# Turning x by crossbar DMA for three of four head pairs in units 3 to 7, with x kept pair-major

## The chip, the cores and the metric

The kernel runs on one core of a Trainium2 chip. The metric is the device time of one execution in microseconds (us); lower is better. Before the change, three runs took 267.28, 267.41 and 268.54 us, a median of 267.41 us.

## What is computed

A block-sparse attention feeds a gated feed-forward layer. q, k and v have shape (4 batches, 8 heads, 768 positions, 64). Reduced to what matters:

```python
k_sum = k.reshape(B, H, 24, 32, D).max(axis=3)
v_sum = v.reshape(B, H, 24, 32, D).mean(axis=3)
# each query: keys less than 16 positions away, and all 24 block summaries (score + log 32)
a = softmax([masked local scores, summary scores])
attn = a @ [v, v_sum]
x = attn.transpose(0, 2, 1, 3).reshape(3072, 512)
g, val = x @ w_gate, x @ w_val               # 512 -> 1536
ffn = (gelu(g) * val) @ w_out                # 1536 -> 512
out = x + sigmoid(x @ w_res) * ffn
```

Because x stands on the left of three products, the kernel needs x twice: with tokens on the partitions (`xn`, for the last line) and with the 512 features on the partitions (`xT`, for the products). The step from `xn` to `xT` is what the change is about.

## The kernel before, in words

**Units.** The 3072 tokens are cut into eight units of 384 tokens (`TU`), two for each batch. A unit has three sub-tiles of 128 tokens (`NSUB`) and four head pairs, each of which gives 128 of the 512 features (`KO` = 4 blocks of features). The main loop (line 454) runs over u from 0 to 7. In iteration u the TensorE (PE) does the feed-forward part of unit u and, mixed into it, the attention of the next unit, n = u + 1. So the x of unit n is made and turned in iteration n - 1; the x of unit 0 is made ahead of the loop, and iteration 7 makes none.

**Feed-forward part of a unit.** For each of 12 feature blocks `fo`, `fo_step` (line 342) runs four matmuls with `w_gate` into `g` and four with `w_val` into `vv` (line 333; the contraction runs over ko = 0 to 3, one head pair of `xT` for each), a Gelu on ScalarE (ACT, line 339) and a product on VectorE (DVE, line 340). After that come, for each sub-tile, `res_step` (four matmuls with `w_res`, line 351, and a tanh, line 357), `ffn_step` (12 matmuls with `w_out`, line 367) and `end_step` (two DVE operations, lines 372 and 374, and the store of 256 KB, line 376, issued on the DMA queue of SyncE, SP). The second of the two DVE operations adds `xn`.

**Attention part.** For each head pair: `s_step` (scores, line 269, and exp, lines 275 and 278), `av_step` (the product with the values, line 301, then `av_norm`: a reciprocal, line 309, and a multiplication that writes the pair's share of `xn`, line 311), and `xt_step`, which turns that pair: three PE transposes of 128 x 128, one for each sub-tile (line 320, into the PSUM tile `xp`), and one ACT copy of 128 x 384 from PSUM to `xT` (line 322).

**Order.** Nothing reorders the work: the order in the text is the order on each engine, and each engine and queue takes its instructions one after the other. Only the semaphore waits are put in from what each instruction reads and writes, and they go by region: an ACT copy of block ko = 3 does not hold back a matmul that reads block ko = 0. In iterations 1 to 6 the order around the change is, after the 12 blocks `fo`: scores 0 and 1; res 0; ffn 0; res 1; av 0 and 1; scores 2 and 3; end 0; six matmuls of ffn 1; xt 0; the other six; xt 1; res 2; av 2 and 3; end 1; seven matmuls of ffn 2; xt 2; three matmuls; xt 3; two matmuls; end 2. Then the next iteration begins with `g` of `fo` = 0, which reads `xT` block by block, ko = 0 first. Iteration 0 has an order of its own and is not touched.

**Buffers.** `xn` and `xT` have two buffers each, so those of unit n were last used by unit n - 2. The PSUM tiles `ao` and `t` are used in turn by `av_step` and `xt_step`; the DMA needs neither.

**Other users of the DMA queues.** The loads of q, k and v for batches 1 to 3 (`load_batch`, line 166, and `load_values`, line 96) are issued by GpSimd (POOL) on its own queue; those for batches 2 and 3 are in the program at the start of iterations 1 and 3, but POOL runs ahead of the PE and issues each as soon as its buffer is free. On SP's queue lie the 26 stores and, at `fo` = 0 of iterations 2 and 4, `turn_batch` (lines 214 and 217): 12 crossbar transposes that turn k and q of batches 2 and 3. They are operations of the same kind as those that the change adds.

Of the kernel before, what the change touches and what calls it, by code (L numbers as in the profile page):

```python
# [9 lines left out]
BF16 = mybir.dt.bfloat16  # L10
AF = mybir.ActivationFunctionType
ALU = mybir.AluOpType
# [3 lines left out]
def kernel(  # L16
# [83 lines left out]
    with tc.manual_schedule():  # L100
# [156 lines left out]
        def s_step(u, hp, st, s=None, two=None, masked=True):  # L257
            b, half = u // 2, u % 2
            first = s is not None
            if two:  # L260
                s = [pool.tile([128, 512], F32, tag=tag, name="s1") for pool, tag in two]
            elif not first:
                s = ps_s.tile([128, 2, 512], F32, tag="s", name="s")
            kw, qt = kW[b % 2][hp], qT[b % 2][hp]
            for t in range(HT):
                tt = half * HT + t
                for hh in range(2):
                    ps = slice(hh * 64, hh * 64 + 64)
                    nc.tensor.matmul((s[hh] if two else s[:, hh])[:, t * QT:(t + 1) * QT], kw[ps, tt, :],  # L269
                                     qt[ps, tt * QT:(tt + 1) * QT], start=not first, stop=True,  # L270
                                     skip_group_check=True)
            P = ppool.tile([128, 2, HT, QT], BF16, tag="P", name="P")
            if two:
                for hh in range(2):
                    nc.scalar.activation(P[:, hh].rearrange("p t q -> p (t q)"), s[hh][:, 0:TU], AF.Exp,  # L275
                                         scale=scale, bias=bias_t[:])
            else:
                nc.scalar.activation(P.rearrange("p a t q -> p a (t q)"), s[:, :, 0:TU], AF.Exp,  # L278
                                     scale=scale, bias=bias_t[:])
            st["P", hp] = P  # L280
            if not first and masked:
                mask_part(hp, st)
# [23 lines left out]
        def av_norm(hp, st):  # L306
            ao = st["ao", hp]
            rz = work.tile([128, NSUB, 2, 1], F32, tag="rz", name="rz")
            nc.vector.reciprocal(rz[:], ao[:, :, :, D:D + 1])  # L309
            xn = st["xn"].rearrange("p s (h d) -> p s h d", d=D)[:, :, 2 * hp:2 * hp + 2, :]  # L310
            nc.vector.tensor_mul(xn, ao[:, :, :, 0:D], rz.to_broadcast([128, NSUB, 2, D]))  # L311

        def av_step(u, hp, st, pool=ps_o, tag="ao"):
# [3 lines left out]
        def xt_step(u, ko, st, pool, tag, copy=nc.vector.tensor_copy):  # L317
            xp = pool.tile([128, TU], BF16, tag=tag, name="xp")
            for sub in range(NSUB):
                nc.tensor.transpose(xp[:, sub * 128:(sub + 1) * 128],  # L320
                                    st["xn"][:, sub, ko * 128:(ko + 1) * 128], ident[:])
            copy(st["xT"][:, ko, :], xp[:])  # L322

        def new_unit():
            return {"xn": upool.tile([128, NSUB, DM], BF16, tag="xn", name="xn"),
                    "xT": upool.tile([128, KO, TU], BF16, tag="xT", name="xT")}

        def half_fo(st, w, fo, lo, hi, acc=None):
# [41 lines left out]
        def end_step(u, st, sub, c0=0, c1=DM):  # L370
            f, th = st["f", sub], st["th", sub][:, c0:c1]
            nc.vector.scalar_tensor_tensor(th, th, 1.0, f[:, 0:c1 - c0], ALU.add, ALU.mult)  # L372
            o = work.tile([128, DM], F32, tag="o", name="o")
            nc.vector.scalar_tensor_tensor(o[:, 0:c1 - c0], th, 0.5, st["xn"][:, sub, c0:c1], ALU.mult, ALU.add)  # L374
            row = u * TU + sub * 128
            nc.sync.dma_start(out=out[row:row + 128, c0:c1], in_=o[:, 0:c1 - c0])

# [76 lines left out]
        for u in range(NU):  # L454
            b, half = u // 2, u % 2
            nb = b + 1
            n = u + 1
            if half == 1 and b + 2 < B:
                load_batch(b + 2)
            gvT = upool.tile([128, FO, TU], BF16, tag="gvT", name="gvT")  # L460
            for fo in range(FO):
                if u == 0 and fo < 2:
                    for w, _, acc in firsts[2 * fo:2 * fo + 2]:
                        half_fo(st, w, fo, KO - 1, KO, acc)
                    fo_end(gvT, fo, firsts[2 * fo][2], firsts[2 * fo + 1][2])
                else:
                    fo_step(st, gvT, fo)
                values_step(u, fo)
                if u == 0 and fo == 4:
                    vext_consts(1)  # L470
                    kw_consts(1)
                    load_batch(1)
                if half == 0 and 1 < nb < B and fo == 0:
                    turn_batch(nb)
                if half == 1 and 1 < nb < B and 0 < fo <= NP:
                    k_rest(kW[nb % 2][fo - 1])
                if u == 1 and fo < 8:
                    home = TT if fo % 2 else AO
                    hp, kq = fo % NP, fo // NP
                    if kq:  # L480
                        q_step(q_sb[nb], nb, 0, S, hp, *home)
                    else:
                        k_step(nb, hp, *home)
                if u == 0 and fo >= FO - 2:
                    for hp in range(2 * (fo - FO + 2), 2 * (fo - FO + 2) + 2):
                        q_step(qb, 0, TU, S, hp, *(TT if hp % 2 else AO))
            nst = new_unit() if n < NU else None
            if u == 0:
                s_step(n, 0, nst)
                s_step(n, 1, nst, two=(AO, TT))  # L490
                r = [res_part(st, sub) for sub in range(NSUB)]
                tanh_part(st, 0, r[0])
                tanh_part(st, 1, r[1])
                tanh_part(st, 2, r[2])
                ffn_step(st, gvT, 0, 0, 4)
                av_step(n, 0, nst, *AO)
                av_step(n, 1, nst, *TT)
                s_step(n, 2, nst)
                s_step(n, 3, nst, two=(MM, MM))
                ffn_step(st, gvT, 1, 0, 4)  # L500
                xt_step(n, 0, nst, *AO, nc.scalar.copy)
                xt_step(n, 1, nst, *TT, nc.scalar.copy)
                ffn_step(st, gvT, 0, 4, 8)
                av_step(n, 2, nst, *AO)
                av_step(n, 3, nst, *TT)
                ffn_step(st, gvT, 1, 4, 8)
                ffn_step(st, gvT, 2, 0, 4)
                xt_step(n, 2, nst, *AO, nc.scalar.copy)
                xt_step(n, 3, nst, *TT, nc.scalar.copy)
                ffn_step(st, gvT, 2, 4, 8)  # L510
                for sub in range(NSUB):
                    ffn_step(st, gvT, sub, 8, FO)
                    end_step(u, st, sub)
                st = nst
                continue
            if nst is None:
                for sub in range(NSUB - 1):
                    res_step(st, sub)
                    ffn_step(st, gvT, sub, 0, FO)
                    end_step(u, st, sub)  # L520
                res_step(st, NSUB - 1)
                for c0, c1 in ((0, 256), (256, 384), (384, DM)):
                    ffn_step(st, gvT, NSUB - 1, 0, FO, c0, c1)
                    end_step(u, st, NSUB - 1, c0, c1)
                continue
            s_step(n, 0, nst)
            s_step(n, 1, nst, two=(AO, TT))
            res_step(st, 0)
            ffn_step(st, gvT, 0, 0, FO)
            res_step(st, 1)  # L530
            av_step(n, 0, nst, *AO)
            av_step(n, 1, nst, *TT)
            s_step(n, 2, nst)
            s_step(n, 3, nst, two=(MM, MM), masked=False)
            end_step(u, st, 0)
            mask_part(3, nst)
            ffn_step(st, gvT, 1, 0, 6)
            xt_step(n, 0, nst, *AO, nc.scalar.copy)
            ffn_step(st, gvT, 1, 6, FO)
            xt_step(n, 1, nst, *TT, nc.scalar.copy)  # L540
            res_step(st, 2)
            av_step(n, 2, nst, *AO)
            av_step(n, 3, nst, *TT)
            end_step(u, st, 1)
            ffn_step(st, gvT, 2, 0, 7)
            xt_step(n, 2, nst, *AO, nc.scalar.copy)
            ffn_step(st, gvT, 2, 7, 10)
            xt_step(n, 3, nst, *TT, nc.scalar.copy)
            ffn_step(st, gvT, 2, 10, FO)
            end_step(u, st, 2)  # L550
            st = nst
# [30 lines left out]
```

The softmax here doesn't subtract the row's maximum and nothing guards it: scores larger than these inputs give would overflow.

## Time and profile before

| what | value |
|---|---|
| median of three runs | 267.41 us |
| the profiled execution's own time | 267.3 us |
| its span, first to last instruction | 265.6 us |
| PE busy | 256.5 us (97%) |
| DVE busy | 167.3 us (63%) |
| ACT busy | 138.8 us (52%) |
| POOL busy | 80.0 us (30%) |
| granted TensorE clock | 1.000 |
| SP's queue, packets' share of the 16 DMA engines | 15.0% |
| POOL's queue, the same share | 67.5% |

"Busy" is the share of the span in which an engine had at least one instruction running. Matmuls overlap in the PE, so the distance between the starts of two successive groups says more about what an instruction costs the PE than its duration does: a duration is the time from start to end of one, a distance is what the next one had to wait. A DMA has two times: how long the issuing queue is occupied, and the time from issue to landing, when its completion is seen.

### The profile page before, as it was taken

How to read it: one execution, taken by the hardware profiler on the slowest of the kernel's cores; microseconds unless marked ns; L12 is line 12 of the kernel's file. 1: busy time of each engine (PE TensorE's matmuls, PEld its weight loads, DVE VectorE, ACT ScalarE, POOL GpSimd, SP SyncE). 2: the span in 40 equal slices, each digit the busy share in tenths (PEclk: the TensorE clock that was granted, in tenths of full speed). 3: DMA queues.
4: the chain of work that ended last, by engine and by line, in shares of the span. 5: the costliest groups of instructions: out<-in, count | busy, mean ns of one | idle time of the engine just before them, and what ended most of it. 6: DMA issues, size and time to landing. Idle time of an engine off the chain costs nothing.

```text
span 265.6 us, 5816 instructions
## 1 busy us (share of the span) xinstructions
PE 256.5 (97%) x2305; PEld 145.1 (55%) x2330; DVE 167.3 (63%) x405; ACT 138.8 (52%) x240; POOL 80.0 (30%) x107
## 2 busy tenths in 40 slices
PE   8799999999999999999999999999999999999994
PEld 2536555566545555556645555556655565556543
DVE  3744863498477877478737866578638853674424
ACT  2745449647565534744365635744365636553310
POOL 7966633998999930040000000000000000000000
PEclk9999999999999999999999999999999999999999
DMA  5999999999999999357001354121001200020012
GB/s 83 172 170 196 197 206 187 141 182 175 119 122 159 188 142 157 54 70 113 2 0 43 107 101 82 31 73 48 2 0 43 79 0 2 18 101 3 2 39 79
DMA packets 90315, 24.50 MB, mean 92 GB/s; under 512 B 76464, under 2 KB 87344, under 8 KB 90288
## 3 DMA queue, kind: packets, MB, share of 16 engines
q0 software_dynamic: 73488, 14.69, 67.5%
q1 hardware_dynamic: 16800, 9.44, 15.0%
q8 instruction: 18, 0.29, 0.5%
q14 instruction: 9, 0.07, 0.1%
HBM read 29.36 MB, written 6.29 MB: 134 GB/s over the span
## 4 chain that ended last, share of the span: by engine, by line
PE 90%; POOL 3%; DMA 3%; issue 1%; DVE 1%; ACT 1%; POOLq 0%; DVEq 0%
PE g L333 23%; PE vv L333 23%; PE f L367 23%; PE r L351 8%; PE ao L301 4%; DMA vext<-in_v_dram 3%; PE s L269 2%; PE vs L227 2%; PE xp L320 2%; POOL vext L96 2%; PE tp L176 1%; PE gv L333 1%; POOL k_sb L87 1%; PE wp L382 1%; DVE th L372 0%
## 5 line engine op out<-in xcount | busy, mean ns | idle before, releaser
L333 PE MATMUL g<-xT,w_gate 128*128 128x384 bf16 x380 | 77.8, 326 | 0.0
L333 PE MATMUL vv<-xT,w_val 128*128 128x384 bf16 x380 | 77.8, 326 | 0.0
L339 ACT ACTIVATE ge<-g 128x384 f32<-128x384 f32 x95 | 46.6, 491 | 58.7 <-DVE gvT L340 31.6
L340 DVE TENSOR_TENSOR gvT<-ge,vv 128x384 bf16<-128x384 f32 x95 | 52.0, 553 | 36.9 <-PE vv L333 33.4
L367 PE MATMUL f<-w_out,gvT 128*128 128x512 bf16 (+2 forms) x298 | 68.6, 362 | 0.7
L333 PEld LDWEIGHTS <-w_val 128*128 128x128 bf16 x384 | 37.6, 98 | 25.4 <-issue 0.5
L333 PEld LDWEIGHTS <-w_gate 128*128 128x128 bf16 x384 | 36.9, 98 | 24.7 <-issue 0.8
L367 PEld LDWEIGHTS <-gvT 128*128 128x128 bf16 x312 | 27.6, 98 | 25.6
L96 POOL DMA_DIRECT2D vext<-in_v_dram x28 | 23.5, 882 | 20.7 <-PE ao L301 20.7
L322 ACT COPY xT<-xp 128x384 bf16<-128x384 bf16 x32 | 15.0, 480 | 22.6 <-PE xp L320 22.6
L351 PE MATMUL r<-w_res,xT 128*128 128x512 bf16 x88 | 24.0, 380 | 0.4
L372 DVE SCALAR_TENSOR_TENSOR th<-th,f 128x512 f32<-128x512 f32 (+2 forms) x26 | 16.7, 642 | 11.4 <-PE f L367 8.5
L286 DVE TENSOR_TENSOR P<-P,maskt 128x768 bf16<-128x768 bf16 x28 | 15.6, 557 | 12.8 <-ACT P L278 10.1
L357 ACT ACTIVATE th<-r 128x512 f32<-128x512 f32 x24 | 14.2, 601 | 17.4 <-PE r L351 17.4
L166 POOL DMA_DIRECT2D k_sb<-in_k_dram x24 | 19.8, 861 | 10.9 <-DMA w_out<-in_moe_w_out_dram 5.2
L166 POOL DMA_DIRECT2D q_sb<-in_q_dram x24 | 19.8, 888 | 0.0
L311 DVE TENSOR_TENSOR xn<-ao,rz 128x384 bf16<-128x384 f32 x32 | 17.8, 558 | 1.1
L278 ACT ACTIVATE P<-s,bias_t 128x768 bf16<-128x768 f32 x18 | 16.2, 902 | 3.3 <-PE s L269 3.2
L374 DVE SCALAR_TENSOR_TENSOR o<-th,xn 128x512 f32<-128x512 f32 (+2 forms) x26 | 16.9, 651 | 0.9
L309 DVE RECIPROCAL rz<-ao 128x6 f32<-128x6 f32 x32 | 6.1, 190 | 18.0 <-PE ao L301 18.0
L275 ACT ACTIVATE P<-s,bias_t 128x384 bf16<-128x384 f32 x28 | 14.6, 577 | 0.0
L351 PEld LDWEIGHTS <-xT 128*128 128x128 bf16 x96 | 8.6, 98 | 8.5
(72 smaller groups left out, 205.3 us busy)
## 6 DMA issues: line engine op xcount, KB each, us to landing
out_dram<-o SPq DMA_DIRECT2D x23, 256.0 KB, 3.2
vext<-in_v_dram POOLq DMA_DIRECT2D x20, 128.0 KB, 5.8
k_sb<-in_k_dram POOLq DMA_DIRECT2D x24, 96.0 KB, 5.7
q_sb<-in_q_dram POOLq DMA_DIRECT2D x24, 96.0 KB, 4.8
w_gate<-in_moe_w_gate_dram POOLq DMA_DIRECT2D x6, 256.0 KB, 8.7
w_val<-in_moe_w_val_dram POOLq DMA_DIRECT2D x6, 256.0 KB, 8.8
w_out<-in_moe_w_out_dram POOLq DMA_DIRECT2D x3, 512.0 KB, 14.1
k_sb<-in_k_dram POOLq DMA_DIRECT2D x2, 384.0 KB, 5.8
```

The costliest lines, as they stand in the source:

```text
L96: nc.gpsimd.dma_start(out=dst, in_=v[b, :, lo:hi, :].rearrange("h p d -> p h d"))
L166: nc.gpsimd.dma_start(out=sb[b][:, h // 2, :, h % 2 * D:h % 2 * D + D], in_=src[b, h].rearrange("(c p) d -> p c d", c=NC))
L278: nc.scalar.activation(P.rearrange("p a t q -> p a (t q)"), s[:, :, 0:TU], AF.Exp, scale=scale, bias=bias_t[:])
L286: nc.vector.tensor_mul(Pf, Pf, maskt.unsqueeze(1).to_broadcast([128, 2 * HT, QT]))
L311: nc.vector.tensor_mul(xn, ao[:, :, :, 0:D], rz.to_broadcast([128, NSUB, 2, D]))
L333: nc.tensor.matmul(acc[:, 0:TU], w[:, ko, fs], st["xT"][:, ko, :], start=(ko == 0), stop=(ko == KO - 1))
L339: nc.scalar.activation(ge[:], g[:, 0:TU], AF.Gelu)
L340: nc.vector.tensor_mul(gvT[:, fo, :], ge[:], vv[:, 0:TU])
L351: nc.tensor.matmul(r[:], st["xT"][:, ko, ss], w_res[:, ko, :], start=(ko == 0), stop=(ko == KO - 1))
L367: nc.tensor.matmul(st["f", sub][:, 0:c1 - c0], gvT[:, fo, ss], w_out[:, fo, c0:c1], start=(fo == 0), stop=(fo == FO - 1))
L372: nc.vector.scalar_tensor_tensor(th, th, 1.0, f[:, 0:c1 - c0], ALU.add, ALU.mult)
L374: nc.vector.scalar_tensor_tensor(o[:, 0:c1 - c0], th, 0.5, st["xn"][:, sub, c0:c1], ALU.mult, ALU.add)
```

## The change

`xn` is laid out pair-major: [128, 4 pairs, 3 sub-tiles, 128] where it was [128, 3 sub-tiles, 512]. All its readers and writers follow: `av_norm`, the PE transposes of `xt_step`, and the last DVE operation of `end_step`, which now reads four runs of 128 elements (fewer for a narrower slice) with a stride between them. A new function `xt_dma` turns one pair with one crossbar DMA transpose issued on SP's queue: in, 128 tokens x (3 sub-tiles x 128 features); out, 128 features x 3 sub-tiles x 128 tokens, straight into `xT`. In iterations 2 to 6 (units 3 to 7) it takes the place of `xt_step` for pairs 0 to 2. Transposes 0 and 1 stand ahead of `end_step` 0, transpose 2 between `av_step` 2 and `av_step` 3. Pair 3 stays on the PE with its ACT copy, as do all four pairs of units 0 to 2.

```diff
-            xn = st["xn"].rearrange("p s (h d) -> p s h d", d=D)[:, :, 2 * hp:2 * hp + 2, :]
+            xn = st["xn"][:, hp].rearrange("p s (h d) -> p s h d", d=D)
...
-                                    st["xn"][:, sub, ko * 128:(ko + 1) * 128], ident[:])
+                                    st["xn"][:, ko, sub, :], ident[:])
...
+        def xt_dma(ko, st):
+            nc.sync.dma_start_transpose(out=st["xT"][:, ko, :].rearrange("d (s m) -> d s m", s=NSUB),
+                                        in_=st["xn"][:, ko].rearrange("p s d -> p (s d)"))
...
-            return {"xn": upool.tile([128, NSUB, DM], BF16, tag="xn", name="xn"),
+            return {"xn": upool.tile([128, KO, NSUB, 128], BF16, tag="xn", name="xn"),
...
-            nc.vector.scalar_tensor_tensor(o[:, 0:c1 - c0], th, 0.5, st["xn"][:, sub, c0:c1], ALU.mult, ALU.add)
+            nc.vector.scalar_tensor_tensor(o[:, 0:c1 - c0].rearrange("p (k d) -> p k d", d=128),
+                                           th.rearrange("p (k d) -> p k d", d=128), 0.5,
+                                           st["xn"][:, c0 // 128:c1 // 128, sub, :], ALU.mult, ALU.add)
...
             s_step(n, 3, nst, two=(MM, MM), masked=False)
+            on_pe = u < 2
+            if not on_pe:
+                xt_dma(0, nst)
+                xt_dma(1, nst)
             end_step(u, st, 0)
             mask_part(3, nst)
             ffn_step(st, gvT, 1, 0, 6)
-            xt_step(n, 0, nst, *AO, nc.scalar.copy)
+            if on_pe:
+                xt_step(n, 0, nst, *AO, nc.scalar.copy)
             ffn_step(st, gvT, 1, 6, FO)
-            xt_step(n, 1, nst, *TT, nc.scalar.copy)
+            if on_pe:
+                xt_step(n, 1, nst, *TT, nc.scalar.copy)
             res_step(st, 2)
             av_step(n, 2, nst, *AO)
+            if not on_pe:
+                xt_dma(2, nst)
             av_step(n, 3, nst, *TT)
             end_step(u, st, 1)
             ffn_step(st, gvT, 2, 0, 7)
-            xt_step(n, 2, nst, *AO, nc.scalar.copy)
+            if on_pe:
+                xt_step(n, 2, nst, *AO, nc.scalar.copy)
             ffn_step(st, gvT, 2, 7, 10)
             xt_step(n, 3, nst, *TT, nc.scalar.copy)
```

## The prediction

> **What bounds the kernel now.** I read the page first: the busy shares and the chain that ended last.
>
> ```profile
> PE 256.5 (97%) x2305; PEld 145.1 (55%) x2330; DVE 167.3 (63%) x405; ACT 138.8 (52%) x240; POOL 80.0 (30%) x107
> PE 90%; POOL 3%; DMA 3%; issue 1%; DVE 1%; ACT 1%; POOLq 0%; DVEq 0%
> ```
>
> The PE is busy for 97% and makes up 90% of the chain; by its waits it loses nothing measurable in the main loop. So whatever leaves the PE shortens the run, and whatever makes the PE wait lengthens it, one for one. What does a turning step cost the PE? Not its duration. Here is the timeline of the PE at the end of iteration 4, where unit 5 is made (start, duration, engine, line, operation).
>
> ```profile
> 175.14 1.68 PE L367 MATMUL f<-w_out,gvT 128*128 128x512 bf16 x6
> 176.66 0.33 PE L320 MATMUL xp<-ident,xn 128*128 128x128 bf16 x3
> 176.83 0.81 PE L367 MATMUL f<-w_out,gvT 128*128 128x512 bf16 x3
> 177.48 0.33 PE L320 MATMUL xp<-ident,xn 128*128 128x128 bf16 x3
> 177.65 0.59 PE L367 MATMUL f<-w_out,gvT 128*128 128x512 bf16 x2
> 178.08 0.81 PE L333 MATMUL g<-xT,w_gate 128*128 128x384 bf16 x4
> 178.73 0.81 PE L333 MATMUL vv<-xT,w_val 128*128 128x384 bf16 x4
> ```
>
> A group of three transposes is followed 0.17 us later by the next group (176.66 to 176.83, 177.48 to 177.65; over all five units the distances are 0.16 to 0.17). I use 0.163. Each transpose "lasts" 0.22 us, but costs 0.054. From the g row: four matmuls in 0.65 us, 0.1625 each; the one that reads ko = 2 starts 0.325 after the row.
>
> When is the third pair's x ready? The DVE timeline of the same iteration; the second multiplication is pair 3's.
>
> ```profile
> 175.06 0.20 DVE L309 RECIPROCAL rz<-ao 128x6 f32<-128x6 f32 x1 [1.10 <-PE ao L301]
> 175.29 0.56 DVE L311 TENSOR_TENSOR xn<-ao,rz 128x384 bf16<-128x384 f32 x1
> 175.98 0.56 DVE L311 TENSOR_TENSOR xn<-ao,rz 128x384 bf16<-128x384 f32 x1
> ```
>
> Pair 2 is ready at 175.29 + 0.56 = 175.85. Its first reader through `xT`, g with ko = 2, starts at 178.08 + 0.325 = 178.405: 2.55 us later. The same distance in the other four units is 2.545 to 2.555.
>
> Last, what a crossbar transpose takes, from the rows of the two kinds that SP already issues (occupation of the queue, minimum/median/maximum in ns) and the line on landing below each.
>
> ```profile
> L217 SPq DMA_TRANSPOSE qT<-q_sb x8: 1209/1210/1308, 93.2 to 165.8; - x8
> DMA to landing us min/median/max: 2.7/2.8/8.2
> ...
> L214 SPq DMA_TRANSPOSE kW<-k_sb x16: 1182/1206/2157, 90.2 to 163.5; - x16
> DMA to landing us min/median/max: 2.3/3.2/7.9
> ```
>
> Both occupy SP for 1.2 us. With no other traffic (iteration 4) a kW transpose, 64 x 768 elements or 96 KB, lands after 2.3 to 2.4 us, with two exceptions of 3.3 and 4.1; a qT one, 128 x 768 or 192 KB, after 2.7 to 2.8. The maxima belong to iteration 2, with POOL's loads in flight. Those loads come again, in the POOL timeline:
>
> ```profile
> 115.92 3.16 POOL L96 DMA_DIRECT2D vext<-in_v_dram  x4 [20.73 <-PE ao L301]
> ```
>
> Four value loads of batch 3 are released by the last `av_step` of iteration 2, just when that iteration's third pair would be turned. No loads come after them.
>
> **What the Trainium skill says.** "VectorE: DVE Perf Modes", section "The three transpose paths", gives 390 ns for a 128 x 128 transpose on TensorE and 1309 ns by crossbar DMA. The trace disagrees on the first in a stream of matmuls (0.054 us of PE time) and has no transpose of one block to compare with the second. "DMA: Bandwidth & Descriptors", section "Queues, rings and completion order", says that each DMA engine alternates between its queues packet by packet. The trace agrees: from 96 to 102 us, with loads on POOL's queue and transposes on SP's, both moved at once:
>
> ```profile
> q0 software_dynamic: 3838, 0.48, 142.8%
> q1 hardware_dynamic: 1865, 0.45, 60.7%
> ```
>
> 0.45 MB in 6 us is 75 GB/s for SP's queue beside the loads.
>
> **The change part by part.**
> *Removed from the PE*: 3 steps x 5 units = 15 steps x 0.163 = 2.45 us, all on the path. This is the whole possible gain, 0.9%.
> *Removed from ACT*: 15 copies x 0.48 us (row L322) = 7.2 us, worth nothing: ACT is busy for 52%. The Gelu table load follows the fourth pair's copy, which stays and moves with the PE. That copy's margin stays too: in iteration 2 it ended at 118.85, and ko = 3 was read at 118.60 + 0.49 = 119.09; both move by the same 0.5 us.
> *Layout*: the `xn` write stays at 384 elements from PSUM (0.56 us). The last DVE operation reads runs of 128; I cost it at nothing. It could lose a little (0.69 now), hidden by DVE's idle 37%; at the kernel's end the slice has 128 columns, one run. No gain, since its inputs are still f32 and bf16.
> *Added on SP*: 15 transposes at up to 1.2 us. Transposes 0 and 1 can go at about 171.0 and 172.2 in iteration 4 (xn 0 and 1 end there at 171.0 and 171.7). Behind them in SP's order stands store 0, which went at 173.52, and transpose 1 leaves SP at about 173.5: a delay under 0.1, of a store that nobody waits for. Both land by 175.1 even at qT's 2.75, 2.5 us ahead of the next g. Transpose 2 waits on pair 2's multiplication; behind it stand stores 1 and 2, which are not ready until about 177.5 (DVE's line 374 ended at 177.86, two steps of 0.163 are gone) and later. `turn_batch` stands behind store 2, and the last of its 12 was issued at 107.14 and 165.83, before transpose 0 of the same iteration. SP is clear. The value loads on POOL go 0.33 us earlier, since two removed steps precede `av_step` 3.
> *Added wait*: g with ko = 2 waits for transpose 2, and all PE work queues behind it, then ACT and DVE. Of the 2.55 us, the removed third step takes 0.163: 2.39. SP starts 0.03 us after its releaser (the store at 114.06 after DVE's end at 114.03); for the PE to resume, which no row shows apart, I set aside 0.05. So the transpose **may take 2.3 us from issue to landing** (2.39 - 0.03 - 0.05); each 0.1 beyond costs 0.1 per unit.
>
> How long does it take? It has 128 partitions in, like qT, but half its columns and bytes: three blocks of 128 x 128 for six. It can't take longer than the whole of qT alone: upper end 2.75. kW of the same bytes: 2.35. In the DMA rows of that time kW's data flow from 1.1 to about 2.0 us after issue, and 0.4 passes until landing. kW and qT occupy SP equally long with the same six blocks of columns; if that goes by blocks, three halve it and the landing drops towards 1.9. I take **2.2**, between: hidden in units 4 to 7, by a small margin.
>
> In unit 3 the data phase (116.04 + 0.03 + 1.1 = 117.2) meets the first value loads, whose packets began at 117.5 before, so 117.2 after. At 75 GB/s, 96 KB take 1.3 us where kW alone took 0.9 and I expect 0.6: 0.4 to 0.7 more, so about 2.9 and a stall of 0.65. Ends: 0, if it slips in ahead; 6.6 (the first kW of iteration 2, with a store ahead of it), a stall of 4.3.
>
> *Sum*: -2.45 + 0.65 = -1.8 us. The profiled execution took 267.3 us (span 265.6 and 1.7 around it), which gives 265.5; it lies 0.1 below the median, 267.41, which gives **265.6 us**.
>
> **The rivals.**
> *B, the third transpose lands late everywhere.* If it behaves like kW or worse (2.4 to 2.75), units 4 to 7 stall by 0.1 to 0.45 each, 0.4 to 1.8 together, and unit 3 by 1.0 to 1.2. Net from 1.05 faster to 0.55 slower: 266.4 to 268.0, 267.1 in the middle. For it: equal bytes took 2.35 already. Against it: half the blocks.
> *C, slower: unit 3's transpose sits behind the value loads.* At 6.6 us it stalls by 4.3, and with transposes as long as qT the other four add 1.8: -2.45 + 6.1 = +3.65, about 271 us. It decides from stalls of 2.45 + 1.34 = 3.8 us in all. For it: landings of 6 to 8 us beside loads in iteration 2. Against it: those stood behind a store and one another; here SP's queue is empty.
> *D, nothing stalls*, the transpose staying ahead of the loads: -2.45, 265.0 us.
>
> **How the numbers follow.** Mine 0.50 (own range 265.0 to 266.4, for unit 3's stall between 0.1 and 1.4), B 0.28, C 0.13, D 0.09. A measurement tells about 0.5%, 1.34 us, from no change: below 266.07 counts as faster, above 268.75 as slower. Faster: nearly all of mine (0.43) and D, 0.52. Slower: C and an edge of B that unforeseen waits push over, 0.15. Within: 0.33. The range takes D's foot and B's end: 264.9 to 268.0, leaving out C and little else.
>
> **What would show it.** Right: 51 transposes on the PE for 96; no PE idle ahead of g in iterations 4 to 7; one wait of PE g on DMA of some 0.6 us near 118.5; landings near 2.2. Wrong: five such waits (B), or one of over 3 us (C). An SP issue well over 1.2 us, or DVE's line 374 well over 0.69 us, would be a cost that I haven't counted.

## The result, and the profile after

The changed kernel takes 271.39 us, the median of four runs (270.11 to 271.74), against 267.57 us for the kernel before, measured beside it. The ratio of the mean times is 1.0128, with a 95% interval of 1.0084 to 1.0172. It is **slower by 1.3%** where I forecast 265.6 us, and it lies outside my range. Timed again later, it took 270.98 us against 267.36, ratio 1.0132 (1.0095 to 1.0168).

The profiled executions took 270.11 us after and 267.3 before. Some runs (two of the four after, four of the five of the shifted stream below) show a lower mean granted clock, 0.991 to 0.994, and are mostly 0.5 to 2 us longer, so below I compare profiles with profiles, which all show 0.997 or more but that of the layout alone (0.991).

The page of the changed kernel: span, busy shares, the chain by engine, and the costliest row of the PE.

```profile
span 268.3 us, 5768 instructions
PE 254.9 (95%) x2285; PEld 142.3 (53%) x2285; DVE 167.3 (62%) x405; ACT 132.3 (49%) x225; POOL 80.1 (30%) x107
...
PE 86%; DMA 7%; DVE 3%; issue 1%; ACT 1%; POOL 1%; POOLq 0%; DVEq 0%
...
L337 PE MATMUL g<-xT,w_gate 128*128 128x384 bf16 x380 | 78.4, 326 | 4.5 <-DMA xT<-xn 4.5
```

The PE has less to do (254.9 us busy for 256.5), yet the span is 2.7 us longer. The last row says where it went: the g matmuls now wait for the DMA of xT. Here is the PE's timeline at the start of the iterations that use units 3, 6 and 7.

```profile
118.07 0.49 PE L337 MATMUL g<-xT,w_gate 128*128 128x384 bf16 x2
121.11 0.48 PE L337 MATMUL g<-xT,w_gate 128*128 128x384 bf16 x2 [2.55 <-DMA xT<-xn]
121.43 0.81 PE L337 MATMUL vv<-xT,w_val 128*128 128x384 bf16 x4
...
208.39 0.49 PE L337 MATMUL g<-xT,w_gate 128*128 128x384 bf16 x2
210.34 0.48 PE L337 MATMUL g<-xT,w_gate 128*128 128x384 bf16 x2 [1.46 <-DMA xT<-xn]
210.66 0.81 PE L337 MATMUL vv<-xT,w_val 128*128 128x384 bf16 x4
...
238.38 0.84 PE L337 MATMUL g<-xT,w_gate 128*128 128x384 bf16 x4
239.06 0.81 PE L337 MATMUL vv<-xT,w_val 128*128 128x384 bf16 x4
```

ko = 0 and 1 run, then ko = 2 stands: the third transpose is late in units 3 and 6, in unit 7 it isn't. Without a stall vv starts 0.65 us after g; what exceeds that is the stall.

| unit | g starts, before | g starts, after | stall at ko = 2 | landing of the third transpose |
|---|---|---|---|---|
| 3 | 118.60 | 118.07 | 2.71 | 5.0 |
| 4 | 147.47 | 149.14 | 0.15 | 2.5 |
| 5 | 178.08 | 179.40 | 0.63 | 3.0 |
| 6 | 206.94 | 208.39 | 1.62 | 3.9 |
| 7 | 235.81 | 238.38 | 0.03 | 2.4 |

The stalls sum to 5.14 us. Between them each unit is shorter by what I had said: from unit 3 to unit 4, 149.14 - 118.07 - 2.71 = 28.36 us, where it took 28.87. So -2.45 + 5.14 = +2.69, and the spans differ by 268.3 - 265.6 = 2.7. Nothing else changed: **the gain is there in full, and the late third transposes take back twice as much.**

The row of the new transposes, and their landing:

```profile
L325 SPq DMA_TRANSPOSE xT<-xn x15: 1179/1182/1852, 111.6 to 236.3; - x15
DMA to landing us min/median/max: 2.3/2.4/5.0
```

2.3 us is the ordinary landing; the deadline was 2.3 us, as worked out. What makes some of them late? In unit 3 the value loads flow beside it. In units 4 to 6 POOL loads nothing. The DMA view of the stretch from unit 6's third transpose, then of the one from unit 7's:

```profile
q8 instruction: 1, 0.02, 1.6%
...
xT<-xn SPq DMA_TRANSPOSE x1, 3.9
...
q1 hardware_dynamic: 421, 0.10, 18.9%
...
xT<-xn SPq DMA_TRANSPOSE x1, 2.4
```

Beside unit 6's there is one packet of 16 KB on queue 8, of the kind "instruction"; beside unit 7's there is none. Going by their kind, such packets bring an engine its instructions (the fetch). Queue 8 has 18 of them, for 4570 PE instructions on the page, some 250 to a packet. A DMA's completion is marked by each of the 16 DMA engines for itself, and the trace holds the marks. In us from each transpose's issue:

| unit | SP occupied | first mark | last mark | instruction packet runs |
|---|---|---|---|---|
| 3 | 1.18 | 3.75 | 5.03 | none; 923 load packets start within 3 us |
| 4 | 1.34 | 2.31 | 2.47 | 0.05 to 0.93 |
| 5 | 1.85 | 2.83 | 2.95 | 0.51 to 1.44 |
| 6 | 1.18 | 2.17 | 3.94 (fifteen by 2.32) | 1.91 to 2.94 |
| 7 | 1.18 | 2.15 | 2.35 | none |

Two patterns: a packet during the issue holds up the issue, and everything with it (in both rows the issue ended 0.41 us after the packet); a packet at the end holds up one engine of the sixteen. There is a third, which none of these five met. Transpose 1 of unit 3 had a packet from 1.49 to 2.45 us after its issue: SP was occupied for the usual 1.20 us, but all sixteen marks came late, from 3.62 to 3.79. It had time, so nothing stalled.

The Trainium skill ("DMA: Bandwidth & Descriptors", section "Why a DMA increments its semaphore by 16 and not by 1") says that the engines of a DMA finish independently and that only the full 16 means landed; unit 6's fifteen marks by 2.32 and one at 3.94 show that here.

### The profile page after: what moved, and what is told of

It reads as the page before. It is cut to its first block, busy times and chain, and to the rows that moved or that the text cites. A ratio compares the mean times of both kernels' runs of the same rounds, so it can differ in the third digit from the quotient of the medians.

```text
span 268.3 us, 5768 instructions
## 1 busy us (share of the span) xinstructions
PE 254.9 (95%) x2285; PEld 142.3 (53%) x2285; DVE 167.3 (62%) x405; ACT 132.3 (49%) x225; POOL 80.1 (30%) x107
## 4 chain that ended last, share of the span: by engine, by line
PE 86%; DMA 7%; DVE 3%; issue 1%; ACT 1%; POOL 1%; POOLq 0%; DVEq 0%
PE vv L337 22%; PE g L337 22%; PE f L371 20%; PE r L355 8%; DMA xT<-xn 4%; PE ao L301 3%; DMA q_sb<-in_q_dram 3%; PE s L269 3%; PE vs L227 3%; PE wp L388 1%; PE tp L176 1%; PE xp L320 1%; DVE gvT L344 1%; DVE xn L311 1%; PE gv L337 1%
## 5 line engine op out<-in xcount | busy, mean ns | idle before, releaser
L371 PE MATMUL f<-w_out,gvT 128*128 128x512 bf16 (+2 forms) x312 | 67.9, 363 | 0.0
L322 ACT COPY xT<-xp 128x384 bf16<-128x384 bf16 x17 | 7.8, 481 | 19.3 <-PE xp L320 19.3
```

The costliest lines, as they stand in the source:

```text
L371: nc.tensor.matmul(st["f", sub][:, 0:c1 - c0], gvT[:, fo, ss], w_out[:, fo, c0:c1], start=(fo == 0), stop=(fo == FO - 1))
```

## The experiments

**Theory:** the loss is the third transpose's lateness and nothing else; loads cause it in unit 3, the PE's own instruction fetch in units 4 to 6. **Rivals:** crossbar transposes vary by themselves; the layout, the SP queue or the traffic cost something apart from the wait.

**The layout alone** (x pair-major, all turns on the PE).

```diff
-            on_pe = u < 2
+            on_pe = True
```

> The changed kernel with x pair-major, but every turn on the PE (on_pe always true), so the layout alone. Theory (the whole loss is the PE waiting on the third transpose): the layout costs nothing, 267.5 us, ratio to before 0.998 to 1.002, and the last DVE operation of end_step stays at 0.69 us. Rival (the layout slows DVE's reads or the PE's weight loads of xn): over 268.3 us, with a longer mean of that DVE row or of the xn multiplication.

267.38 us, ratio 1.0012 (0.9996 to 1.0028); line 378, the last DVE operation, has a median of 691 ns, as before. The layout costs nothing that shows.

**Two pairs by DMA, the third back on the PE.**

```diff
-                xt_dma(2, nst)
...
-            if on_pe:
-                xt_step(n, 2, nst, *AO, nc.scalar.copy)
+            xt_step(n, 2, nst, *AO, nc.scalar.copy)
```

> Transposes 0 and 1 by DMA in units 3 to 7, pairs 2 and 3 on the PE. Theory: these two have over 5 us from issue to use, so no PE wait on a DMA is seen, and 10 steps of 0.163 us go: 267.5 - 1.6 = 265.9 us. Rival (the transposes cost something besides the wait: SP's order, traffic that slows others, a lower granted clock): 267 us or more, without a PE wait on xT.

265.65 us, ratio 0.9932 (0.9909 to 0.9956): 1.7 us faster, and no PE wait on a DMA of xT. Of its ten transposes three landed after 3.2 to 3.4 us, which nobody notices where issue and use lie over 5 us apart. So transposes cost nothing where they have time, and a removed step is worth the 0.163 us.

**From unit 4 on only.**

```diff
-            on_pe = u < 2
+            on_pe = u < 3
```

> The changed kernel, but DMA only from unit 4 on, so that no transpose meets the value loads. Theory (two causes: unit 3 meets the loads, 2.5 us; others are hit when a 16 KB packet of the PE's own instruction fetch runs beside them, up to 1.6 us each): 12 steps x 0.163 = 2.0 us less, one or two units hit (which ones can change, since the PE has 18 instructions more ahead of unit 4), 0.5 to 2.2 us: 266.0 to 268.0 us. Rival (a crossbar transpose beside matmuls simply varies between 2.3 and 5 us): stalls of 1 us and more in any of the four units, without a fetch packet near, 268 to 269.5 us. Rival (only the value loads matter): no stalls above 0.2 us, 265.7 us.

266.56 us, ratio 0.9966 (0.9955 to 0.9976). Unit 5 stalls by 1.16 us (a packet from -0.24 to 1.55 us of its issue), unit 6 by 0.27 (0.11 to 1.07), units 4 and 7 not at all, and no packet runs beside theirs. As the theory says; "only the loads" is out.

**The last four value loads of batch 3 held back.** They are issued in iteration 3, behind a POOL copy that has to wait for that iteration's first gvT block.

```diff
-            for c in range(NC + 1):
+            for c in range(NC + 1 if b < 3 else HT // 2):
                 load_values(b, c)
...
+                if u == 3 and fo == 1:
+                    nc.gpsimd.tensor_copy(late[:], gvT[:, 0, 0:2])
+                    for c in range(HT // 2, NC + 1):
+                        load_values(3, c)
```

> The changed kernel, with the last four value loads of batch 3 held back on POOL by a small copy that reads the first gvT block of iteration 3, so that they start about 4 us after unit 3's third transpose should have landed. Theory (the loads delay unit 3's transpose by 2.5 us): its stall falls from 2.6 to between 0 and 1.6 us (an instruction fetch of the PE runs near it too), the others stay: 268.8 to 270.0 us against 271.4. Rival (the transpose of unit 3 is late for another reason, the fetch or the transpose itself): the stall stays near 2.6 us and the time at 271.4 us.

268.2 us, ratio 1.0036 (1.0017 to 1.0055). Its PE timeline at unit 3, where the changed kernel stood for 2.55 us, and at unit 6:

```profile
118.30 0.81 PE L338 MATMUL g<-xT,w_gate 128*128 128x384 bf16 x4
118.95 0.81 PE L338 MATMUL vv<-xT,w_val 128*128 128x384 bf16 x4
...
208.21 0.48 PE L338 MATMUL g<-xT,w_gate 128*128 128x384 bf16 x2 [1.63 <-DMA xT<-xn]
```

Unit 3's stall is gone, all of it, more than I expected; the loads were its whole cause. The other units' stalls stay (0.41, 0.43, 1.79, 0.04).

**The PE's instruction stream shifted.** Sixty-four short matmuls, each with its weight load, go in ahead (128 instructions), and two warm-up matmuls go out.

```diff
-        keep_warm(13, wp)
+        keep_warm(11, wp)
+        for i in range(64):
+            nc.tensor.matmul(wp[:, 0:64], warm[:, 0:128], warm[:, 0:64], start=True, stop=True)
```

> The changed kernel, with 64 short matmuls (64 columns, zeros, in the PE's idle time before the first k arrives; 2 of the 13 warm-up matmuls go) put in ahead, which moves the PE's instruction stream by 128 instructions, half of a 16 KB fetch packet. They compute nothing that is used. Theory (the stalls of units 4 to 6 come from fetch packets that run beside the third transpose): the packets move by half a packet's distance, all third transposes of units 4 to 7 land after 2.3 to 2.4 us, and only unit 3's stall from the value loads, 2.5 us, stays: 267.6 to 268.6 us against 271.4. Rival (transposes vary by themselves, or something else than the fetch holds them): stalls of 0.4 to 1.8 us in units 4 to 6 as before, 270 to 271.5 us.

269.45 us, ratio 1.0067 (1.0042 to 1.0091). The PE at unit 3 and at unit 6, then SP's timeline at the last unit's first two transposes:

```profile
122.02 0.48 PE L337 MATMUL g<-xT,w_gate 128*128 128x384 bf16 x2 [2.40 <-DMA xT<-xn]
...
208.52 0.81 PE L337 MATMUL g<-xT,w_gate 128*128 128x384 bf16 x4
209.17 0.81 PE L337 MATMUL vv<-xT,w_val 128*128 128x384 bf16 x4
```

```profile
230.45 3.74 SPq L325 DMA_TRANSPOSE xT<-xn  x2
```

Units 4 to 6 have no stall any more (0.00 each), unit 3 keeps its 2.6. The packets now meet transposes 0 (here the issue of one took 2.44 us, so two took 3.74), which have time. The packet that ran beside unit 6's third transpose, the fifteenth on queue 8, came at 208.26 us in the changed kernel and comes at 202.21 here, though that transpose is issued within 0.13 us of the same time. That the packets move with the PE's instruction count also says whose they are. The time is above the 267.6 to 268.6 us that I expected: the profiled execution took 268.61 us, the others 269.12 to 269.68. The short matmuls themselves put the first g of iteration 1 at 55.4 us, 0.7 later, which I had left out.

**Both at once.**

> The late value loads and the shifted instruction stream together. Theory (loads and fetch are the whole of it): every third transpose lands after 2.3 to 2.4 us, no stall above 0.1 us, and the predicted gain of 2.45 us comes out: 264.9 to 265.6 us against 267.4 before. Rival (another cost is left, such as the added waits or the traffic): over 266.3 us though no transpose is late.

265.39 us, ratio 0.9919 (0.9893 to 0.9945), 2.0 us faster than before, and no PE wait on a DMA of xT; the stalls of the five units sum to 0.07. Loads and fetch are the whole of the loss, and the predicted gain exists.

**Pair 2's av moved ahead.**

```diff
             ffn_step(st, gvT, 1, 0, 6)
+            if not on_pe:
+                av_step(n, 2, nst, *AO)
+                xt_dma(2, nst)
...
-            av_step(n, 2, nst, *AO)
-            if not on_pe:
-                xt_dma(2, nst)
+            if on_pe:
+                av_step(n, 2, nst, *AO)
             av_step(n, 3, nst, *TT)
```

> The changed kernel, with av of pair 2 and its transpose moved ahead, to where the first turning step stood (behind six matmuls of ffn 1), in iterations 2 to 6. That gives the transpose 2.3 us more until its use, 4.6 us in all, and it lands ahead of the value loads. Theory (only the deadline was too tight): landings of up to 4.1 us beside a fetch no longer stall the PE, 264.9 to 265.6 us. Rival (the transposes cost PE time in another way, or the early av waits for its mask and stalls the PE): over 266.3 us.

267.79 us, ratio 1.0009 (0.9994 to 1.0023): a miss of mine, for two reasons. The PE timeline of iteration 2:

```profile
110.62 1.47 PE L371 MATMUL f<-w_out,gvT 128*128 128x512 bf16 x6
112.10 0.38 PE L301 MATMUL ao<-vext,P 128*64 128x65 bf16 x12
112.42 1.47 PE L371 MATMUL f<-w_out,gvT 128*128 128x512 bf16 x6
```

Six f take 1.30 us, so av could have gone at 111.92; it went at 112.10, when DVE's mask of that pair ended (112.05), and two groups of 12 cost 0.63 where one of 24 took 0.51. That is 0.3 us per unit, 1.5 in all. And DVE does end 0 and a mask ahead of the pair's multiplication, which ends at 114.54: 3.55 us ahead of its use, not 4.6. In this iteration SP lost some of that too: a fetch packet ran during the issue of store 0, which took 1.49 us (0.53 in the next two), so the transpose went at 115.18. Stalls of 1.12, 0.50 and 0.30 us remain in units 3 to 5.

**Pair 3 by DMA as well** in units 4 to 7.

```diff
+            if u >= 3:
+                av_step(n, 3, nst, *TT)
+                xt_dma(3, nst)
             res_step(st, 2)
...
-            xt_step(n, 3, nst, *TT, nc.scalar.copy)
+            if u < 3:
+                xt_step(n, 3, nst, *TT, nc.scalar.copy)
```

> As the one with av of pair 2 early, and in iterations 3 to 6 pair 3 goes by DMA as well, its av moved ahead of res 2; 19 steps are gone from the PE in place of 15. Theory: -0.65 us more if pair 3, which has about 3.3 us until its use, is hit by no fetch packet at its end; av 3 may wait 0.1 us for its mask: 264.3 to 265.5 us. Rival (pair 3 meets fetch packets, one engine late by up to 1.8 us): stalls of 0.3 to 1 us in one or two units, no better than 265.2 us.

270.24 us, ratio 1.0101 (1.0074 to 1.0128). Stalls of 1.85, 0.70 and 0.86 us in units 3 to 5 and the same early av; at the very end the last DVE operation waited 1.40 us for an earlier store, which this one profile alone shows. That store landed after 3.64 us, where its like took 2.01 in the changed kernel, and a fetch packet ran from 0.66 to 2.09 us after its issue. Worse than the rival's figure too.

**The third transpose read last.** Pair 2 by DMA from unit 4 on, with ko = 2 of g 0, vv 0 and g 1 behind the rest of all three.

```diff
+        def two_fo(st, gvT):
+            todo = [(w_gate, 0), (w_val, 0), (w_gate, 1)]
...
+            for w, fo in todo:
+                acc = half_fo(st, w, fo, 0, 2)
+                ko_part(st, w, fo, acc, 3, False)
+                accs.append(acc)
+            for (w, fo), acc in zip(todo, accs):
+                ko_part(st, w, fo, acc, 2, True)
...
+                elif u >= 4 and fo == 0:
+                    two_fo(st, gvT)
...
-            if not on_pe:
+            if u >= 3:
                 xt_dma(2, nst)
```

> Pairs 0 and 1 by DMA in units 3 to 7, pair 2 by DMA in units 4 to 7 only, and in iterations 4 to 7 the first three groups of a unit (g 0, vv 0, g 1) run ko = 0, 1 and 3 first and ko = 2 of all three last, which gives the third transpose 7 matmuls more, 7 x 0.1625 = 1.1 us, 3.5 us in all. Theory (a deadline of 3.5 us covers a transpose that a fetch makes late, mostly): 10 + 4 steps are gone, 14 x 0.163 = 2.3 us less, and at most one or two stalls of under 0.6 us: 265.0 to 265.9 us against 267.4. Rival (reading ko = 2 last delays the first Gelu and stalls the PE on a PSUM buffer, or the fetch stalls stay): above 266.3 us.

265.34 us, ratio 0.9914 (0.9893 to 0.9936): 2.0 us faster than the kernel before. No other median is lower, though that of both at once, 265.39, is too close to call. Unit 6's third transpose landed after 4.0 us, and the PE waited for it 0.4.

**Two pairs from unit 2 on.**

```diff
-            on_pe = u < 2
+            on_pe = u < 1
...
-            if not on_pe:
-                xt_dma(2, nst)
...
-            if on_pe:
-                xt_step(n, 2, nst, *AO, nc.scalar.copy)
+            xt_step(n, 2, nst, *AO, nc.scalar.copy)
```

> Pairs 0 and 1 by DMA from unit 2 on, pairs 2 and 3 on the PE; unit 2 is turned in iteration 1, in the midst of the loads of batch 2. Theory (beside the loads a transpose takes 4 to 8 us, and these two have 5.5 to 6.8 us): 12 steps gone, 1.96 us less, but a stall of 0 to 2.5 us in iteration 2: 265.4 to 267.9 us. Rival (an SP queue without a backlog keeps it under 5 us even beside the loads, as in unit 3): no stall, 265.4 us.

266.11 us, ratio 0.9935 (0.9911 to 0.9960). Amid the loads of batch 2 the two transposes landed after 6.15 and 6.44 us and stalled the PE by 0.99 us, three times the 0.33 us that the two more saved steps give.

**The changed kernel again.**

> The changed kernel again, unaltered, for its time beside the others of this call and for a second profile. Theory (the fetch packets come at the same place of the instruction stream each time, and so do the value loads): again no stall in unit 7, again the longest in unit 3 and stalls in units 5 and 6, 270 to 271.5 us. Rival (the late transposes are chance): other units are hit.

270.98 us. Stalls of 2.90, 0.51, 0.18, 1.48 and 0.03 us: the same units, the same order of size for the two large ones. It isn't chance.

All the traces together speak against the rival that crossbar transposes vary by themselves. They hold 157 transposes of xT. The 71 that had neither loads nor an instruction packet beside them landed after 2.28 to 2.38 us, every one. The 79 with a packet and no loads took up to 4.11, and the seven beside loads 3.98 to 6.44.

## Why the prediction was wrong

- *The bound and the gain*: right. Fifteen steps x 0.163 us are gone from the PE, and each stall-free stretch is shorter by that; two pairs alone gave 1.7 us for an expected 1.63.
- *Layout, ACT, SP's order*: right, nothing that shows (layout alone 1.0012; store 0 went at 114.21 in iteration 2, for 114.06 before).
- *The deadline of 2.3 us*: right. A landing of 2.35 in unit 7 left 0.03 us of stall, one of 2.47 in unit 4 left 0.15.
- *The transpose's ordinary landing*: 2.3, where I took 2.2. SP's occupation doesn't go by blocks: 1.18 us for three of them, 1.2 for six. Small by itself, but it used up the margin.
- *Unit 3 beside the value loads*: **the failed step**. The place was right, and the loads' packets began at 117.14. The size was not: I charged nothing but the slower flow of the data and made 2.9 us of landing and 0.65 of stall from it (from 2.9 it would be 0.6); it was 5.0 and 2.71. The rate itself held fairly well: the 96 KB flowed in 1.57 us, or 63 GB/s, and in the second profile of the same kernel in 1.37 us, or 72, where I had taken 75. Against unit 7's transpose this flow took 0.94 us more. Two delays I had put at nothing: the first data packet came 1.72 us after the issue in place of 1.16, 0.56 more, and from the last data packet to the landing 1.74 us passed in place of 0.56, 1.18 more. The three make the 2.68 us by which it landed later. With pair 2 moved ahead, unit 3's data had flowed by 1.95 us after the issue, nearly as fast as alone, and still landed after 3.98. Why the marks come so late beside loads no run settles. My bound of 6.6 us did contain it.
- *Units 4 to 6*: **the step that was missing.** I called them hidden; they stalled by 0.15 + 0.63 + 1.62 = 2.4 us. The instruction fetch was in no part of my sum and in none of the rivals. What the runs showed in its place: a fetch packet beside each of the three, and no stall once the packets had moved away. Of the 4.5 us of stall beyond my 0.65, 2.06 fall in unit 3 and 2.43 in units 4 to 7. It could have been seen: I wrote "with two exceptions of 3.3 and 4.1" and left them at that. The DMA view of the kernel before, from 161.8 to 166 us, where the two fall, has this:

```profile
q8 instruction: 1, 0.02, 2.2%
q14 instruction: 1, 0.01, 1.8%
...
kW<-k_sb SPq DMA_TRANSPOSE x2, 3.7
```

- *The rivals*: C had the right sign and named the right place, at 4.3 us for unit 3; its other four stalls were to come from long transposes and came from fetches. Its limit, 3.8 us of stalls, was passed (5.14). That its 271 us is so near the measured time is luck in part: 4.3 us stood for 2.71 and 1.8 for 2.43. B's transpose that is late everywhere is out: with nothing beside it, none landed after more than 2.38 us.

## What to carry to other kernels

When a wait on a DMA takes the place of work on the bound engine, set its deadline against the late landings of that kind of DMA, not the ordinary ones, and look up what ran beside each exception, the instruction queues too. A transfer with over 5 us from issue to use was free here, away from the loads of a batch; one with 2.3 cost twice what it saved. If the deadline is tight, move the use: reading the late block last gave 1.1 us at no cost that shows, while moving its source ahead cost 0.3 us per unit.

## What the runs showed of the hardware that I had not expected

- The PE's instructions are fetched in packets of 16 KB (18 in the program) over the DMA engines that serve transfers. What one did to a crossbar transpose without loads beside it depended on when it began, counted from the transpose's issue:
  - From 0.25 us before to 0.61 after (19 cases): in 17 of them the issue, 1.18 us without a packet, ended 0.40 to 0.43 us after the packet did; at most it took 2.44.
  - From 0.99 to 1.49 us (nine cases): the issue took its usual 1.18 to 1.20 us, but all sixteen marks were late, and the landing came 1.31 to 1.34 us after the packet's end.
  - From 1.75 to 2.04 us (five cases): fifteen marks came on time, and the last 1.0 to 1.2 us after the packet's end, up to 1.8 us late (4.11 for 2.3, with the loads held back). The packets of 8 KB on queue 14 did this last too, by 0.9 us (3.2 for 2.3 at several transposes 0).
  - From 2.27 us on: nothing; with none but such a packet beside it, a transpose landed after 2.33 to 2.34 us.
- So an edit that only changes how many instructions the PE has can move a stall from one place to another: in the shifted kernel, 64 more matmuls with their weight loads at the start removed 2.4 us of stalls.
- A crossbar transpose of 128 x 384 occupies SP for 1.18 us and lands after 2.3 us; beside the value loads, in the changed kernel's order, 4.9 to 5.2, and amid the loads of a batch, 6.1 to 6.4.
